# Idle matmuls in planned waits, padded loads of v and a new table of places in an attention and two-layer mixture kernel on one core

## The chip, the cores and the metric

The kernel runs on one NeuronCore of a Trainium2 chip, in one launch. The metric is the device time of that core in microseconds; the time before is the median of three runs. Five engines work side by side, each in its own program order: TensorE (PE; its weight loads are shown as PEld), VectorE (DVE), ScalarE (ACT), GpSimd (POOL) and SyncE (SP), which issues every DMA.

## What is computed

```python
def reference(q, k, v, moe_w_in, moe_w_out, moe_a, moe_b, moe2_phi, moe2_w1, moe2_w2):
    # attention, 4 x 8 heads, 576 positions, 64 wide:
    # means of 4 positions attend to each other (144 x 144), repeated 4 times,
    # plus attention over the positions less than 4 away
    x = (out_up + out_local).transpose(0, 2, 1, 3).reshape(2304, 512)
    h = x @ w_in                                   # 512 -> 2048
    P = a[0] + a[1] * h + a[2] * h**2 + a[3] * h**3
    Q = 1.0 + abs(b[0]) * abs(h) + abs(b[1]) * h**2
    x = (P / (Q + 1e-06)) @ w_out                  # 2048 -> 512
    # soft mixture of 8 experts with 4 slots each
    logits = x @ phi
    d, c = softmax(logits, 0), softmax(logits, 1)
    slots = d.T @ x                                # 32 x 512
    out = c @ [relu(slots[e] @ w1[e]) @ w2[e] for e in range(8)]
```

## The kernel before

**Stages.** Sixteen attention units (four batches, two heads side by side on the 128 partitions) come first. Each is a `pair`: banded scores of nine 64-row tiles (`sc0`, `sc1`), scores of the pooled heads (`scd`), the peak (DVE), the exponential (ACT), the norm, transposes of the probabilities (`tp0` to `tp2`, `td0`, `td1`), products with v (`avd`, `av`) and the sum `x`, split into a high and a low part (`XH`, `XL`). Four units make one `XH`/`XL` of 512 tokens. The first four units have buffers of their own (the four `Set`s); the other twelve take turns in set A. Between them, eight pieces of `w_in` are cut from 64-bit words by DVE and split into `W0` to `W7` (`split_in`), and eight of `w_out` likewise (`split_out`), stored to a scratch in HBM and folded with phi into `wphi`.

**The middle.** `h` multiplies a pair of `W` columns with 512 tokens (24 matmuls into two banks, `hps`, L757 of the profile), and eleven steps on ACT, DVE and POOL make the rational function of it (`ab`, `cr`, `v`, `a`, `t`, `p`, `ln`, `ex`, `e`, `nL`, `gL`, L819 to L842). The results are transposed (`tr`, L867) and copied out (`gc`, L608 on ACT or L610 on DVE) and summed into logits (`lg`). `route` does the softmax over tokens as it goes: `lt`, `tk`, and `dsp` (L939), which adds a group of tokens to the 32 slots.

**The end.** `sl` multiplies the slots with w_out (`Wo`), `l1` with the experts' w1 (`hp`, L1171), `l2` with w2 (`op`, L1292), and `o` combines. w1 and w2 come in 32 loads of 1 MB (`we`) into buffers of the middle, as these fall free, and 19 stores (`out`) end the program.

**What sets the order.** Every piece of work is entered by `at` with its reads, writes and PSUM bank. `Plan.order` sorts all of them by the table `PLACE` (one number for each piece), so the order on each engine is written in that table; the strings in `F` choose the engine of a piece (a for ACT, d for DVE, p for POOL), one letter for each unit or block. `order` also runs through the pieces with the costs in `PARTS` and keeps a clock of TensorE of its own (`fast`, `tick`), by which it hands out the three shared PSUM banks. SP's loads wait in SP's own order.

**What the change touches.** `F`, `PLACE`, `FILL` and `PARTS`; `order` and `emit` (L232 on); `load_v` (L416), which fetches v twice, as 72 rows for pooling (`vd`) and as 70 rows of windows (`vw`); `logits` (its bank `lg`); `fillers` (L1002), matmuls on a cleared tile, 44 of them, all ahead of the first `h`; `turn_c` and `keep_c`, the transposes of the combine weights late in the program; and in `kernel` the arrays `vw` and `vd`.

Of the kernel before, what the change touches and what calls it, by code (L numbers as in the profile page):

```python
# [29 lines left out]
    pq="ddppdddddddppppp",  # L30
    pk="ppddddppddpddddd",
    pv="pppppdpppppppppp",
    nl="dppppddpppppdppp",
    nd="dddppppddpdppdpp",
    wih="aaadaaaa",
    wil="pdpppppp",
    xh="aaaaadaadaaaddadd",
    xl="pdpdpppdppppddppd",
    v="ppddpppddpddpdppppdppdpppppddpppdppdp",
    e="ddddddddddddddddddddddddddddddddddddd",  # L40
    cr="adaaaadaaaaadaaaaaddaaaddaddaaaaaaaaa",
    a="daaaaaddaaaaaaadadaadadaadadaadaaadaa",
# [66 lines left out]
    cr=(407, 277, 451, 329, 528, 501, 627, 585, 675, 696, 735, 778, 819, 848, 882, 917, 939, 973, 998, 1053, 1088,
        1114, 1146, 1175, 1194, 1208, 1230, 1269, 1276, 1307, 1320, 1343, 1368, 1395, 1407, 1440, 1445),  # L110
    v=(412, 282, 483, 334, 538, 508, 632, 589, 681, 703, 739, 788, 824, 852, 888, 919, 945, 981, 1008, 1062, 1095,
        1122, 1153, 1178, 1196, 1214, 1232, 1274, 1282, 1312, 1325, 1348, 1373, 1403, 1412, 1447, 1450),
    a=(415, 262, 442, 467, 541, 535, 609, 623, 665, 720, 758, 774, 818, 851, 880, 918, 943, 965, 997, 1034, 1076,
        1108, 1154, 1173, 1193, 1213, 1229, 1245, 1268, 1301, 1321, 1337, 1359, 1380, 1405, 1433, 1453),
    t=(419, 266, 459, 473, 547, 540, 616, 641, 670, 728, 763, 780, 823, 861, 889, 921, 948, 982, 1014, 1047, 1085,
        1116, 1157, 1177, 1195, 1216, 1234, 1251, 1277, 1303, 1326, 1344, 1361, 1384, 1409, 1438, 1456),
    p=(424, 281, 465, 480, 576, 543, 635, 647, 685, 732, 768, 801, 834, 865, 896, 928, 957, 994, 1024, 1063, 1104,
        1119, 1163, 1182, 1198, 1217, 1236, 1258, 1286, 1315, 1328, 1347, 1367, 1386, 1413, 1449, 1466),
    ln=(422, 294, 485, 341, 546, 516, 645, 594, 686, 713, 743, 797, 828, 855, 900, 927, 953, 990, 1010, 1070, 1103,
        1130, 1158, 1185, 1200, 1218, 1240, 1279, 1284, 1324, 1331, 1353, 1385, 1411, 1419, 1451, 1455),  # L120
    ex=(426, 297, 489, 347, 550, 520, 649, 597, 689, 717, 749, 804, 833, 864, 903, 930, 960, 1002, 1021, 1077, 1117,
        1135, 1161, 1187, 1202, 1220, 1248, 1281, 1291, 1327, 1334, 1363, 1387, 1414, 1420, 1467, 1458),
# [30 lines left out]
    we=(1378, 1339, 1338, 1352, 1355, 1463, 1495, 1459, 1492, 1375, 1371, 1392, 1432, 1423, 1428, 1425, 1510, 1509,  # L153
        1487, 1496, 1488, 1528, 1521, 1527, 1518, 1526, 1534, 1536, 1530, 1539, 1535, 1533),
    zm=(1205,),
    gst=(1512,),
    inv=(1505,),
    gt0=(1513,),
    gt1=(1514,),
# [1258 lines left out]
```

## Time and profile before

| | |
|---|---|
| time, median of 3 runs | 556.72 us (555.61 to 557.39) |
| the profiled execution, its own time | 560.98 us |
| its span, first to last instruction | 558.9 us |
| mean granted TensorE clock | 0.935 |
| busy: PE, DVE, ACT, POOL | 499.3, 469.8, 331.6, 175.8 us |
| moved by DMA | 83.83 MB, 150 GB/s in the mean |

All durations below come from the profiled execution. [...] A busy PE is not PE at its peak, since the ends of matmuls are modelled.

### The profile page before, as it was taken

The numbers are of one execution on the slowest core, as the hardware profiler recorded it, in microseconds if no ns is written. First come the engines' busy times: TensorE is split into PE (matmuls) and PEld (weight loads), VectorE is DVE, ScalarE is ACT, GpSimd is POOL, SyncE is SP. The second block draws the span as 40 slices with busy tenths as digits, with TensorE's granted clock in tenths as the row PEclk, the third lists the DMA queues.
The fourth block names the chain that finished last, engine by engine and source line by source line (L and its number), as shares of the span: only waits on it lengthen the run. The fifth ranks groups of instructions, "written<-read, shape, count | busy, mean of one in ns | idle before, by whom it ended". The sixth has DMA issues, their size and how long they took to land.

```text
span 558.9 us, 10661 instructions
## 1 busy us (share of the span) xinstructions
PE 499.3 (89%) x4332; PEld 355.6 (64%) x4332; DVE 469.8 (84%) x618; ACT 331.6 (59%) x636; POOL 175.8 (31%) x130
## 2 busy tenths in 40 slices
PE   7799889678887979799999989999999999769995
PEld 4466667456665757576778767677775798323465
DVE  5687999889989899888999999999999999962523
ACT  4356554755774554877787665676658868820122
POOL 2637085537331151500254442243410313000100
PEclk9899997767996989989999999999999999789998
DMA  8986543221234543102002020024000096899977
GB/s 231 216 348 199 211 155 150 88 88 64 99 114 156 158 135 137 44 37 65 24 2 88 23 87 1 24 75 189 39 1 0 2 344 259 333 385 420 420 302 288
DMA packets 16705, 83.83 MB, mean 150 GB/s; under 512 B 1968, under 2 KB 2480, under 8 KB 10000
## 3 DMA queue, kind: packets, MB, share of 16 engines
q1 hardware_dynamic: 16656, 83.15, 42.4%
q8 instruction: 34, 0.56, 0.4%
q14 instruction: 15, 0.12, 0.1%
HBM read 74.23 MB, written 8.91 MB: 149 GB/s over the span
## 4 chain that ended last, share of the span: by engine, by line
PE 48%; DVE 28%; ACT 10%; DMA 9%; issue 3%; SPq 1%; POOL 0%; ACTq 0%; DVEq 0%
PE hps L757 19%; PE gt L867 4%; DMA at<-in_qk 3%; DVE gate L841 3%; PE dsp L939 3%; DVE wst L639 3%; DVE gate L825 3%; DMA at<-in_vd 2%; PE hp L1171 2%; PE sc L459 2%; PE lg L883 2%; PE op L1292 2%; DVE wo L643 2%; DVE gate L839 2%; DVE gate L842 2%
## 5 line engine op out<-in xcount | busy, mean ns | idle before, releaser
L757 PE MATMUL hps<-XH,W 128*128 128x512 f32 x512 | 177.1, 412 | 3.1 <-DVE A L836 2.1
L757 PEld LDWEIGHTS hps<-XH,W 128*128 128x128 f32 x512 | 99.7, 195 | 31.4 <-issue 3.9
L825 POOL TENSOR_TENSOR gate<-gate 128x1024 f32<-128x1024 f32 x23 | 59.5, 2589 | 158.7 <-ACT gate L819 112.0
L757 PE MATMUL hps<-XL,W 128*128 128x512 f32 x256 | 102.9, 402 | 0.0
L757 PEld LDWEIGHTS hps<-XL,W 128*128 128x128 f32 x256 | 49.9, 195 | 9.1
L837 ACT ACTIVATE gate<-gate,one 128x1024 f32<-128x1024 f32 (+1 forms) x37 | 41.9, 1131 | 22.5 <-POOL gate L825 16.6
L841 DVE SCALAR_TENSOR_TENSOR gate<-gate,one 128x1024 f32<-128x1024 f32 (+1 forms) x37 | 50.3, 1359 | 4.8 <-ACT gate L838 4.8
L828 ACT ACTIVATE gate<-hps 128x1024 f32<-128x1024 f32 (+1 forms) x37 | 37.2, 1005 | 18.8 <-PE hps L757 9.4
L482 ACT ACTIVATE at<-sc,at 128x70 f32<-128x70 f32 x144 | 32.9, 333 | 22.6 <-DVE at L476 12.7
L838 ACT ACTIVATE gate<-gate 128x1024 f32<-128x1024 f32 (+1 forms) x37 | 38.4, 1038 | 0.6
L497 POOL TENSOR_TENSOR at<-at 128x630 f32<-128x630 f32 (+1 forms) x21 | 25.1, 1194 | 39.4 <-DVE at L493 39.3
L608 ACT COPY G<-gt 128x512 f32<-128x512 f32 x53 | 30.7, 586 | 7.5 <-PE gt L867 7.3
L819 ACT ACTIVATE gate<-gate,cf_sb 128x1024 f32<-128x1024 f32 (+1 forms) x28 | 34.1, 1218 | 0.5
L842 DVE SCALAR_TENSOR_TENSOR gate<-gate 128x1024 f32<-128x1024 f32 x24 | 32.6, 1358 | 0.6
L839 DVE SCALAR_TENSOR_TENSOR gate<-gate,cf_sb 128x1024 f32<-128x1024 f32 x24 | 32.1, 1341 | 0.2
L502 PE MATMUL tp<-cf_sb,at 128*70 128x128 f32 x144 | 25.5, 307 | 6.6 <-DVE at L543 2.8
L505 ACT COPY at<-tp 70x512 f32<-70x512 f32 (+1 forms) x48 | 21.8, 476 | 16.1 <-PE tp L502 15.9
L836 DVE SCALAR_TENSOR_TENSOR gate<-gate,cf_sb,hps 128x1024 f32<-128x1024 f32 x24 | 30.6, 1275 | 0.4
L867 PE MATMUL gt<-cf_sb,gate 128*128 128x128 f32 x192 | 29.8, 286 | 1.2 <-DVE X L543 0.9
L459 PEld LDWEIGHTS sc<-at 64*64 64x64 f32 x576 | 22.0, 143 | 13.9 <-issue 9.2
L825 DVE TENSOR_TENSOR gate<-gate,hps 128x1024 f32<-128x1024 f32 x24 | 29.2, 1215 | 0.9 <-ACT gate L828 0.6
L459 PE MATMUL sc<-at 64*64 64x70 f32 x576 | 26.9, 238 | 3.1 <-DMA at<-in_qk 3.1
(158 smaller groups left out, 992.7 us busy)
## 6 DMA issues: line engine op xcount, KB each, us to landing
we<-in_w SPq DMA_DIRECT2D x32, 1024.0 KB
at<-in_qk SPq DMA_DIRECT2D x16, 579.0 KB
wst<-in_w_in SPq DMA_DIRECT2D x8, 1024.0 KB
wst<-in_w_out SPq DMA_DIRECT2D x8, 1024.0 KB
at<-in_vw SPq DMA_DIRECT2D x16, 315.0 KB
at<-in_vd SPq DMA_DIRECT2D x16, 288.0 KB
out<-late SPq DMA_DIRECT2D x17, 256.0 KB
wo_dram<-wo SPq DMA_DIRECT2D x8, 512.0 KB
```

The costliest lines, as they stand in the source:

```text
L459: nc.tensor.matmul(t[r, i - i0, :], lhsT=s.qT[r, 64 * i:64 * i + 64], rhs=s.kT[r, 64 * i:64 * i + WIN], start=False, stop=True, skip_group ...
L482: nc.scalar.activation(out=dst[:, i, :], in_=st["s", j][:, i, :], func=ACTF.Exp, scale=scale, bias=mx[:, i:i + 1], accum_out=sm[:, i:i + 1 ...
L757: nc.tensor.matmul(hps[m][:, c].rearrange("p u t -> p (u t)"), lhsT=W[p][:, w, kk, 128 * c:128 * c + 128], rhs=x[xx][:, kk, :], start=(kk ...
L819: act(out=out, in_=x, func=ACTF.Identity, scale=coef[:, w:w + 1], bias=coef[:, b:b + 1])
L825: (nc.vector if who == "d" else nc.gpsimd).tensor_tensor(out=out, in0=x, in1=y, op=ALU.mult)
L828: do("ab", "B", "H", lambda B, H: act(out=B, in_=H, func=ACTF.Abs))
L837: do("ln", "C", "B", lambda C, B: act(out=C, in_=B, func=ACTF.Ln, bias=one))
L838: do("ex", "C", "", lambda C: act(out=C, in_=C, func=ACTF.Exp, scale=-1.0))
L839: do("n", n, P + "C", lambda n, P, C: stt(out=n, in0=P, scalar=coef[:, 0:1], in1=C, op0=ALU.add, op1=ALU.mult), part="nL" if kept == "2" e ...
L841: do("e", "B", "C", lambda B, C: stt(out=B, in0=B, scalar=one, in1=C, op0=ALU.add, op1=ALU.mult), pick=("e", m))
L842: do("g", "A", "B" + n, lambda A, B, n: stt(out=A, in0=B, scalar=-2.0, in1=n, op0=ALU.add, op1=ALU.mult), part="gL" if n == "A" else "g")
L867: nc.tensor.transpose(gt[n][:, u, 128 * c:128 * c + 128], g_of(n, c)[:, 128 * u:128 * u + 128], idn)
```

## The change

1. **Idle matmuls.** `order` drops its clock of TensorE and counts matmuls at full speed after the first 5.3 us of the plan. Wherever the plan sees TensorE wait over 0.6 us, it notes a number of idle matmuls, (wait - 0.35) / 0.083, and `emit` puts them ahead of the waiting piece. Each is 128x192 in bf16 on a tile of zeros, adds to the upper half of the logits' bank, and waits for nothing. There are 245 (20 of them at the very start), for 44 of 128x512 before.
2. **v in 80 rows.** The arrays `vd` and `vw` get rows of zeros up to 80, and `load_v` fetches 80 rows. What is computed still reads 72 and 70.
3. **A new table.** `PLACE` has new numbers throughout, and `F` other engines for some pieces. DVE loses six `gc` copies, three `a`, two whole and two half `v` multiplies, two norm scalings, two `XH` casts, the casts of one `W` and of the last block's x, and that block's subtraction; it gains two `W` subtractions, two of `XL` and one pooling of v. ACT gets the copies, casts and `a`; POOL the `v` multiplies.
4. **Banks.** `LG` is one tile for the whole program, and `turn_c` takes one of the three shared banks, not the logits'.

```diff
 F = dict(
...
-    gc="aadadaadaaaaaaaaaaaaaaaaaddadaadaadaadadaaaadadaaaadaaaaaadaaaadadaaaddd",
+    gc="aaaadaaaaaaaaaaaadaaaaadaaaaaaddadadaaadaaaaaadaaaadaaaaaaaaaaaaaaaaaddd",
...
-    ldqk=(2, 3, 4, 7, 19, 161, 210, 271, 332, 378, 425, 549, 706, 777, 906, 1001),
+    ldqk=(2, 4, 5, 7, 21, 151, 213, 268, 325, 369, 407, 556, 698, 761, 893, 965),
...
-FILL = (12, 2, 4, 0, 8, 0, 2, 0, 0, 0, 8, 4, 4)
+FILL = (10,) + (0,) * 12
...
-    ldqk=dict(sp=1.7), ldv=dict(sp=2.3), ldi=dict(sp=2.8), ldo=dict(sp=2.8), sto=dict(sp=1.6), ldc=dict(sp=.5),
+    ldqk=dict(sp=1.8), ldv=dict(sp=3.0), ldi=dict(sp=2.8), ldo=dict(sp=2.8), sto=dict(sp=1.6), ldc=dict(sp=.5),
...
-                rows, now = self.rows.get(before, 1.0), t
-                while us > 1e-6:
-                    while tick <= now:
-                        fast, busy, tick = busy >= .42 * TICK, 0.0, tick + TICK
-                    rate = 1.0 if fast else 0.5
-                    step = min(us / rate, tick - now)
-                    now, us, busy = now + step, us - step * rate, busy + step * rate * rows
-                us = now - t
+                if t - free[e] > .6:
+                    self.idles[n] = int((t - free[e] - .35) / .083)
+                us *= 1.0 if t > 5.3 else 2.0
...
         for n in self.order(banks):
             self.now = self.place.get(n)
+            if n in self.idles:
+                self.idle(self.idles[n])
             self.items[n][5](*self.items[n][6])
...
+    LG = psum.tile([128, 2 * TB], F32, tag="lg", name="lg")
...
+            self.Vl, self.Vdl = v[0:80], self.Vd[0:80]
...
-        nc.sync.dma_start(out=s.Vd, in_=vd[bb, p])
-        nc.sync.dma_start(out=s.V, in_=vw[bb, p].rearrange("r (t c) -> r t c", t=9))
+        nc.sync.dma_start(out=s.Vdl, in_=vd[bb, p])
+        nc.sync.dma_start(out=s.Vl, in_=vw[bb, p])
...
-            nc.tensor.matmul(fill, lhsT=acc.bitcast(BF16)[:, 0:128], rhs=acc.bitcast(BF16)[:, 0:512], start=True, stop=True)
+            nc.tensor.matmul(fill[:, 0:192], lhsT=zero[:, 0:128], rhs=zero, start=not used, stop=True,
+                             skip_group_check=True)
+            used.append(n)
...
-        mid["c"] = psum.tile([128, 4, 128], F32, tag="lg", name="ct", bufs=1)
+        mid["c", u] = bank("ct", shape=(4, 128))
...
+    def rows80(x):
+        return np.pad(x, [(0, 0), (0, 0), (0, 80 - x.shape[2]), (0, 0)])
```

Three places of the order. **TensorE, in the attention units of the second batch**, ahead of the blocks that use `W2`: `av` is the product with v, `tp` and `tpd` are transposes of probabilities, `sc` and `scd` scores. Before:

```order
L529 MATMUL avd<-at 64x144 x4
L522 MATMUL avd<-at 64x64 x2
L522 MATMUL av<-at 64x64 x16
L502 MATMUL tp<-cf_sb,at 70x128 x8
L510 MATMUL tpd<-cf_sb,at 72x128 x6
```

and in the change:

```order
L526 MATMUL avd<-at 64x144 x4
L519 MATMUL avd<-at 64x64 x2
L519 MATMUL av<-at 64x64 x16
L1004 LDWEIGHTS zero
L1004 MATMUL lg<-zero 128x192
...
L499 MATMUL tp<-cf_sb,at 70x128 x4
L507 MATMUL tpd<-cf_sb,at 72x128 x3
```

Behind this `av` stand 39 idle matmuls, the longest run. From here to the first use of `W2` there are 24, 7, 4 and 25 more; in all, 61 stand ahead of the first `h` and 184 behind it.

**TensorE at the end of the middle**, where the last groups of tokens go to the slots (`dsp`), the sum is transposed (`gst`) and multiplied with w_out (`sl`). Before:

```order
L930 MATMUL tok<-cf_sb,L 128x32 x2
L939 MATMUL dsp<-G,DC 32x512 x8
L1111 MATMUL gst<-cf_sb,acc 128x128 x4
L1125 MATMUL sl<-Wo,GT 32x512 x16
L1143 MATMUL si<-cf_sb,GT 128x32 x4
```

and in the change:

```order
L927 MATMUL tok<-cf_sb,L 128x32 x2
L936 MATMUL dsp<-G,DC 32x512 x8
L1004 LDWEIGHTS zero
L1004 MATMUL lg<-zero 128x192
...
L1115 MATMUL gst<-cf_sb,acc 128x128 x4
L1004 LDWEIGHTS zero
L1004 MATMUL lg<-zero 128x192
...
L1129 MATMUL sl<-Wo,GT 32x512 x16
```

Ahead of this `dsp` stand 3, 15 and 5 idle matmuls, and behind it 7, 11, 5 and 3 up to the first expert matmul, where there was none.

**SP, the loads of the experts' weights** (`we`) and the reload of w_out (`Wo`). Before:

```order
L1044 DMA Wo<-wo_dram 128x2048 x4
L976 DMA we<-in_w 128x2048 x14
L980 DMA we<-in_w 128x2048 x2
L976 DMA we<-in_w 128x2048 x2
L980 DMA we<-in_w 128x2048 x14
```

and in the change:

```order
L973 DMA we<-in_w 128x2048
L1048 DMA Wo<-wo_dram 128x2048 x4
L973 DMA we<-in_w 128x2048 x13
L977 DMA we<-in_w 128x2048
L973 DMA we<-in_w 128x2048 x2
L977 DMA we<-in_w 128x2048 x15
```

One load of 1 MB moves ahead of the four of `Wo`; the other 31 keep their side of it.

## Rows read from the trace of the kernel before

**Rows 1.** The page: busy time of each engine; the granted clock in 40 slices.

```profile
PE 499.3 (89%) x4332; PEld 355.6 (64%) x4332; DVE 469.8 (84%) x618; ACT 331.6 (59%) x636; POOL 175.8 (31%) x130
...
PEclk9899997767996989989999999999999999789998
```

**Rows 2.** Stretches: us, PE, PEld, DVE, ACT, POOL busy, clock, DMA share, GB/s.

```profile
75.00:100.00 25.00, 22.31 (x215) 17.08 (x213) 22.56 (x32) 13.66 (x32) 15.43 (x11) 0.86 0.37 137
100.00:125.00 25.00, 16.87 (x183) 12.66 (x183) 21.73 (x33) 15.19 (x43) 11.55 (x7) 0.66 0.31 99
125.00:150.00 25.00, 20.74 (x161) 15.57 (x162) 24.16 (x32) 16.03 (x30) 16.20 (x11) 0.86 0.26 90
150.00:200.00 50.00, 41.56 (x299) 30.49 (x297) 43.93 (x45) 29.50 (x51) 11.02 (x7) 0.90 0.39 122
...
250.00:300.00 50.00, 50.00 (x400) 35.69 (x399) 45.48 (x57) 37.65 (x70) 12.53 (x10) 1.00 0.15 43
...
400.00:450.00 50.00, 49.70 (x306) 36.51 (x299) 49.02 (x47) 37.20 (x51) 9.95 (x5) 1.00 0.06 19
...
475.00:490.00 15.00, 12.14 (x90) 5.48 (x92) 14.15 (x19) 12.80 (x28) 0.00 (x0) 0.77 0.87 338
...
510.00:520.00 10.00, 8.98 (x85) 3.13 (x78) 2.81 (x9) 0.00 (x0) 1.85 (x1) 1.00 1.01 419
```

**Rows 3.** The chain that ended last, in order of time: start us, us, what.

```profile
3.46 13.45 DMA at<-in_vd
...
61.38 2.74 PE hps L757 x12
...
174.49 5.23 PE hps L757 x12
...
258.58 1.85 PE dsp L939 x16
...
317.96 3.26 DVE gate L842
...
481.35 3.64 PE dsp L939 x16
...
497.04 3.53 PE dsp L939 x16
```

**Rows 4.** Groups on DVE by shape: busy us, mean ns | idle before.

```profile
L842 DVE SCALAR_TENSOR_TENSOR gate<-gate 128x1024 f32<-128x1024 f32 x24 | 32.6, 1358 | 0.6
...
L825 DVE TENSOR_TENSOR gate<-gate 128x1024 f32<-128x1024 f32 x12 | 15.8, 1320 | 0.9 <-ACT gate L819 0.9
...
L610 DVE COPY G<-gt 128x512 f32<-128x512 f32 x19 | 13.0, 683 | 0.1
...
L821 DVE TENSOR_SCALAR gate<-hps,cf_sb 128x1024 f32<-128x1024 f32 x9 | 12.1, 1339 | 0.8 <-ACT gate L828 0.5 <-PE gt L867 0.2
...
L497 DVE TENSOR_TENSOR at<-at 128x432 f32<-128x432 f32 x7 | 6.9, 997 | 0.0
...
L613 DVE TENSOR_TENSOR XL<-at,XH 128x512 fp32r<-128x512 f32 x5 | 3.4, 674 | 0.0
...
L443 DVE TENSOR_REDUCE at<-at 72x256 f32<-72x1024 f32 x1 | 2.0, 1956 | 0.0
...
L613 DVE TENSOR_TENSOR W<-wst,W 128x1024 fp32r<-128x1024 f32 x1 | 1.2, 1216 | 0.0
```

**Rows 5.** The timeline of the start: one run of the old fillers.

```profile
16.73 1.90 PE L1004 MATMUL fill<-acc 128*128 128x512 bf16 x8
```

**Rows 6.** DMA of the first 30 us in 40 slices, and packets of the whole program.

```profile
GB/s 0 0 117 323 420 340 334 340 377 327 272 159 182 194 189 190 209 193 170 170 202 246 211 201 204 206 197 220 137 251 193 216 224 160 242 232 377 349 407 412
...
DMA packets 16705, 83.83 MB, mean 150 GB/s; under 512 B 1968, under 2 KB 2480, under 8 KB 10000
```

**Rows 7.** Short stretches, columns as in rows 2.

```profile
109.22:112.63 3.41, 3.20 (x29) 1.85 (x27) 3.38 (x4) 1.95 (x5) 1.59 (x1) 0.50 0.00 0
```

More of the change, by code (lines that the diff above doesn't have):

```diff
@@ L29 @@
 F = dict(
[L30 to L39, printed above, removed]
+    pq="pppddddpdddpppdd",
+    pk="pppdddpdddddddpd",
+    pv="pppppppppdpdpppp",
+    nl="dppdppdppppppppp",
+    nd="ppppdddddpppdppp",
+    wih="aaaaaaaa",
+    wil="pddppdpp",
+    xh="aaaaaaaaaadaaadda",
@@ L153 @@
[L153 to L159, printed above, removed]
-    sl=(1516,),
-    si0=(1519,),
-    si1=(1520,),
-    si=(1522,),
-    z=(1523,),
-    l1=(1524, 1525, 1529, 1531, 1532, 1537, 1542, 1545),
-    z2m=(1540,),
-    hs0=(1548,),
-    hs1=(1549,),
-    ht=(1552,),
@@ L185 @@
-    out=(1594, 1591, 1597, 1604, 1609, 1588, 1602, 1607, 1617, 1624, 1625, 1633, 1638, 1640, 1644, 1647, 1653, 1650,
-        1652),
+    dm=(0,),
+    ldqk=(2, 4, 5, 7, 21, 151, 213, 268, 325, 369, 407, 556, 698, 761, 893, 965),
+    ldc=(1, 3),
+    ldv=(6, 8, 11, 23, 122, 228, 289, 337, 379, 439, 589, 655, 837, 935, 990, 1090),
+    coef=(50,),
+    pq=(9, 17, 28, 61, 120, 198, 230, 291, 343, 390, 423, 567, 724, 844, 923, 1015),
+    pk=(13, 22, 33, 77, 123, 201, 236, 321, 346, 392, 428, 593, 751, 857, 948, 1059),
@@ new lines @@
+    wc0=(144, 237, 508, 546, 577, 629, 682, 716),
+    wt1=(150, 242, 498, 544, 580, 624, 685, 715),
+    wc1=(155, 245, 501, 548, 585, 626, 689, 719),
+    wp=(161, 261, 511, 549, 591, 632, 699, 721),
+    wpp=(167, 265, 514, 552, 594, 638, 702, 725),
+    wq=(187, 267, 534, 573, 596, 643, 705, 737),
+    wpc=(188, 272, 537, 576, 600, 646, 707, 749),
+    ldi=(14, 30, 27, 203, 216, 234, 271, 153),
+    wih=(149, 199, 232, 260, 332, 374, 411, 455),
+    wil=(156, 210, 241, 269, 336, 396, 417, 464),
@@ new lines @@
+    lgc=(764, 966, 1224, 1392, 1485),
+    lt=(771, 799, 987, 1018, 1229, 1256, 1400, 1432, 1486),
+    L=(782, 807, 994, 1027, 1244, 1266, 1410, 1445, 1489),
+    mx=(779, 803, 992, 1020, 1231, 1270, 1407, 1447, 1490),
+    al=(788, 822, 996, 1026, 1258, 1318, 1435, 1463, 1497),
+    E=(787, 808, 998, 1028, 1246, 1274, 1415, 1459, 1492),
+    ss=(790, 864, 1010, 1191, 1273, 1356, 1455, 1474, 1508),
+    tk=(798, 809, 1004, 1040, 1250, 1281, 1426, 1462, 1494),
+    dt=(800, 812, 1009, 1043, 1252, 1283, 1436, 1464, 1496),
@@ new lines @@
+    ds=(804, 817, 1012, 1109, 1269, 1300, 1439, 1469, 1498),
+    ac=(810, 827, 1023, 1118, 1277, 1343, 1450, 1495, 1499),
+    wor=(1179,),
+    h8=(1332, 1337, 1328, 1345, 1354, 1369, 1348, 1359, 1372, 1391, 1378, 1387, 1408, 1412, 1402, 1421),
+    we=(1160, 1323, 1325, 1376, 1352, 1452, 1482, 1449, 1479, 1375, 1364, 1399, 1401, 1418, 1427, 1431, 1501, 1500,
+        1484, 1478, 1487, 1522, 1519, 1524, 1520, 1517, 1518, 1523, 1525, 1527, 1530, 1529),
+    zm=(1350,),
+    gst=(1503,),
+    inv=(1509,),
@@ new lines @@
+    gt0=(1504,),
+    gt1=(1505,),
+    sl=(1507,),
+    si0=(1510,),
+    si1=(1511,),
+    si=(1512,),
+    z=(1513,),
+    l1=(1515, 1516, 1521, 1526, 1528, 1531, 1535, 1538),
+    z2m=(1533,),
+    hs0=(1541,),
+    hs1=(1542,),
+    ht=(1546,),
+    z2=(1550,),
+    c1=(1502,),
+    c2=(1506,),
+    c3=(1514,),
+    cs=(1532, 1539, 1537, 1545, 1548),
+    ct=(1534, 1543, 1540, 1549, 1551),
+    cc=(1536, 1547, 1544, 1554, 1553),
+    l2=(1552, 1555, 1556, 1557, 1558, 1559, 1561, 1562, 1560, 1563, 1565, 1567, 1569, 1571, 1577, 1587, 1579, 1592,
+        1599, 1605, 1607, 1609, 1614, 1616),
@@ L187 @@
+    os=(1564, 1590, 1619),
+    s4=(1566, 1595, 1621),
+    s4h=(1568, 1598, 1624),
+    s4l=(1570, 1604, 1625),
+    o=(1585, 1573, 1580, 1575, 1589, 1596, 1572, 1582, 1602, 1611, 1612, 1618, 1623, 1628, 1629, 1632, 1638, 1640,
+        1635),
+    out=(1591, 1583, 1594, 1581, 1597, 1606, 1600, 1603, 1610, 1620, 1617, 1626, 1631, 1633, 1637, 1641, 1644, 1646,
+        1645),
 )
 IDLE = (0, 0)
-FILL = (12, 2, 4, 0, 8, 0, 2, 0, 0, 0, 8, 4, 4)
+FILL = (10,) + (0,) * 12
 PIECES, SHORT = 2, 1
@@ L260 @@
     issues = dict(ldv=2, wor=4)
-    rows = dict(sc0=.75, sc1=.75, scd=.85, av=.65, avd=.5, lg=.8, lt=.65, o=.55, wp=.85, wq=.13, si=.13, ht=.13, tk=.07, tr=.8,
-                tp0=.8, tp1=.8, tp2=.8, td0=.8, td1=.8, wt0=.8, wt1=.8, ct=.8, gst=.8)
     wait = dict(pe=.2, act=.14, dve=.13, pool=.14, sp=0.0)
@@ L270, in order @@
         owner, moved, self.place = [None] * banks, 0.0, {}
-        fast, busy, tick, before, shared = False, 0.0, TICK, None, 0.0
+        before, shared, self.idles = None, 0.0, {}
         count = {}
@@ L998, in attn_moe_moe_kernel @@
     sets = [A, Set(1, "G0", "G1", "G2", "G3"), Set(2, "g0", "g1", "g2", "g3"), Set(3, "w4", "w5", "w6", "w7")]
-    fill = psum.tile([128, 512], F32, tag="lg", name="fill", bufs=1)
+    fill = LG[:, TB:]
+    used = []
+    zero = const.tile([128, 192], BF16, name="zero")
+    nc.vector.memset(zero, 0.0)
     def fillers(n):
         for _ in range(n):
-            nc.tensor.matmul(fill, lhsT=acc.bitcast(BF16)[:, 0:128], rhs=acc.bitcast(BF16)[:, 0:512], start=True, stop=True)
+            nc.tensor.matmul(fill[:, 0:192], lhsT=zero[:, 0:128], rhs=zero, start=not used, stop=True,
+                             skip_group_check=True)
+            used.append(n)
+    plan.idle = fillers
     nc.vector.memset(acc, 0.0)
     if FILL[0]:
-        at(-100, "DM", "dm", fillers, FILL[0], w=["lg"], scale=FILL[0])
+        at(-100, "DM", "dm", fillers, 2 * FILL[0], w=["id"], scale=FILL[0])
     def load_cb():
@@ L1274, in keep_c @@
         dst = room(7, [128, 16, 128], F32R)[:, u:u + n] if u < 16 else mid["ct"]
-        nc.scalar.copy(out=dst, in_=mid["c"][:, 0:n, :])
+        nc.scalar.copy(out=dst, in_=mid["c", u][:, 0:n, :])
     for j in range(5):
@@ L1280, in attn_moe_moe_kernel @@
         tail("cs", "cs", split_c, u, n, t=t, r=["DC", ("done", 4 if j == 0 else 5)], w=[("cs", j)])
-        tail("ct", "ct", turn_c, u, n, t=t, r=[("cs", j)], w=["lg"], scale=n / 4)
-        tail("cc", "cc", keep_c, u, n, t=t, r=["lg", ("done", 3), *(["L"] if j == 4 else [])], w=[("CT", j)])
+        tail("ct", "ct", turn_c, u, n, t=t, r=[("cs", j)], ps=("ct", j), scale=n / 4)
+        tail("cc", "cc", keep_c, u, n, t=t, r=[("ct", j), ("done", 3), *(["L"] if j == 4 else [])], w=[("CT", j)])
     so = {}
```

195 lines of the change are left out of this document (76 added, 119 removed), and 14 rows, old and new, of tables (gc, tr).

## The prediction

> **What bounds the kernel now.** I read the page first, then the stretches, then the chain. On the page [rows 1] TensorE is busy 89% of the span and VectorE 84%, ScalarE 59% and GpSimd 31%: two engines are near full, the other two have room. The clock row beside it says that a busy TensorE is not always a fast one: its lowest digits, 6 and 7, lie between the 7th and the 13th of the 40 slices (84 to 182 us) and at the 35th (475 us).
>
> The stretches [rows 2] tell who is the limit where. [...] From 250 to 450 us TensorE is busy all the time at full clock (50.00 of 50 us, and 49.70 at the end of it) with VectorE at 45.48 to 49.02 of 50: both are the limit, and no clock is left to win. From 475 to 490 the clock falls to 0.77. From 510 on DMA is full (share 1.01, 419 GB/s) with the experts' weights.
>
> [...]
>
> **The change part by part.** The sum is made against the profiled execution, 560.98 us, which lies 4.26 us (0.8%) above the median of 556.72 us and above all three timed runs; what I find is taken off the median.
>
> *Work taken off VectorE.* At the prices of [rows 4]: six copies of G at 0.683 (4.10), three linear steps at 1.339 (4.02), two `v` at 1.320 (2.64), two halves of it (1.32), two norm scalings, priced as the 432-element one, 0.997 (1.99), four casts at no more than the 0.674 of the `XL` row (2.70), and one subtraction like W's, 1.216: 18.0 us go. Two subtractions of W (2.43), two of XL (1.35) and one pooling of v (1.96) come: 5.7. Net 12.3 us of VectorE's 469.8, most of it between 75 and 490 us, where it bounds. ScalarE takes the copies and linear steps in its 41% of free time; that cover would be gone only where TensorE waits for a copied G. Gain between 0 (TensorE holds 250 to 450 us anyway) and 12.3; I take two thirds, **-8**, since in all stretches from 75 to 200 us VectorE is the fuller engine.
>
> *Clock in the middle.* [...] But the end gains at most what VectorE is idle there, 12.6 us, and part of those holes is other waiting. Between 0 and -12.6 I take the middle, **-6**; what is late next is VectorE, with W2 to W7 still to be cut.
>
> *Clock near the end.* Two `dsp` at 1.85 save 1.8 + 1.7 = 3.5 us, and both stand on the chain. Behind them the loads of weights limit: DMA is full at 510 us. The load that moves ahead of `Wo` takes 1 MB off that queue, 1.05 MB / 419 GB/s = 2.5 us. So between 0 (loads land no earlier) and -5.5 (3.5, and more from the transposes there) I take **-3**.
>
> *What the idle matmuls cost.* One old filler of 512 columns took 1.90 / 8 = 0.237 us at full clock [rows 5]; 192 columns by the same rate are 0.089 us, an estimate. The 61 ahead of the first `h` (5.4 us) replace 44 old ones (10.4 us). The 184 behind it are 16.4 us of work with no use. They wait for nothing, so they run in the wait that the plan saw, if it is there: the largest place, 39 + 24 + 7 + 4 + 25 = 99 of them, 8.8 us, lies in the stretch from 100 to 135 us, where TensorE was idle for 25 - 16.87 = 8.1 us in the first 25 us alone, and would be idle for more at full clock. In the last part some are tight: 11 of them are 1.0 us between `gst` and `sl`. Between 0 and +16.4 I take **+2**.
>
> *Loads of v.* The start waits for DMA: the chain has 13.45 us for a load of v [rows 3]. While the 128-row loads stand alone the core moves 320 to 420 GB/s; once v's 72 and 70 rows come, at about 8 us, it moves 160 to 250 [rows 6]. Two bounds for 80 rows. If the rate of the 128-row loads came back, the first four units' v (80 rows of 4096 and 4608 bytes each) would take 2.79 MB / 340 = 8.2 us instead of 2.47 MB / 200 = 12.3 for 72 and 70 rows: -4.1. If the rate stays, 0.32 MB more takes 1.6 us: +1.6. Eighty rows are far nearer to 72 than to 128, so I take **0**, the side on which the zeros cost no more than they bring. [...]
>
> *The table and the banks.* Which piece is late is new everywhere. An order can save or lose VectorE's idle time and no more than a like amount; from the 12.6 us above I give it 6 either way and take **0**. The bank of `turn_c` is nothing: those transposes lie between matmuls that DMA bounds.
>
> Sum: -8 - 6 - 3 + 2 + 0 + 0 = -15, or 546 us for such an execution as was profiled, and 556.7 - 15 = **542 us** for the median.
>
> **The rivals.**
> - *VectorE keeps the clock's gain* (chance 0.20). TensorE gets faster, but VectorE, full to 87 to 97% from 75 to 200 us, waits for its own loads and for GpSimd. For it: one multiplication in the chain took 3.26 us [rows 3] against a mean of 1.358 [rows 4], so VectorE can be held up, and more products now go to GpSimd. Against: the chain has slow matmuls in it. Then -8 - 1 + 2 remain: 549 us.
> - *All of it comes* (0.14): -12 - 8 - 4 + 1 - 2 = -25, 532 us.
> - *The idle matmuls stand in the way* (0.17, slower). TensorE takes its work in order; behind an idle run waits the `tp` or `h` that VectorE and ScalarE need next. Place: the 99 between the seventh unit's `av` and W2, and the 46 from the last `dsp`s to the experts. If the waits are not where the plan has them, 16.4 us are paid at full clock and near twice that at half, for 6 + 3 us of clock. It decides once more than the gain of VectorE's relief and the clock, 17 of 16 to 33 us, is paid. With 21 us paid: 556.7 - 17 + 21 = 561 us.
> - *The clock falls all the same and the rest evens out* (0.09, no change). From 109.2 to 112.6 us TensorE was busy for 3.20 of 3.41 us, with transposes, scores and small products, at clock 0.50 [rows 7]; no wait stood there, so the plan puts nothing there. Then -6 and -3 fall out, +2 stays, and of the relief 3 us, since slow TensorE work hides the rest: 555.7 us. [...]
>
> **How the numbers follow.** The forecast near 542 (537 to 547) has 0.40, the rivals 0.20, 0.14, 0.17 and 0.09. A measurement of this kernel can tell about 0.3%, 1.7 us, from no change. Faster: 0.40 + 0.20 + 0.14 and a little of the last, 0.75; the same 0.08; slower 0.17. The range leaves out the slower case and the far half of the best: 530 to 557 us.
>
> **What would show it.** Right: clock near 1.00 from 75 to 200 and from 475 to 500 us; all `dsp` at about 1.85 us; VectorE busy near 457 us; 245 idle matmuls at about 0.09 us, with TensorE's waits in front of W2 shorter by their time. The v loads still at 160 to 250 GB/s in the start. Wrong: clock digits under 9 again between 100 and 135 us; VectorE idle for more than 13 us from 75 to 200 us, behind TensorE; `sl` or the first `hp` starting only when idle matmuls end; or a DMA share of 1 for longer than before at the end, which would take the tail's 3 us.

## The result and the profile after

| | before | after |
|---|---|---|
| median | 556.46 us (4 runs, 555.61 to 557.39) | 535.41 us (4 runs, 531.26 to 539.37) |
| ratio | | 0.9596, 95% interval 0.9527 to 0.9666 |
| profiled execution | 560.98 us, span 558.9 | 539.37 us, span 537.3 |

The changed kernel is 21 us faster; 15 were forecast, and 535.4 lies in the range of 530 to 557. Two later sets of runs of the same kernel gave 0.9621 and 0.9607. The ratio leaves out one slow run of the four after, 539.37 us, which is also the profiled execution; the profiled one of before lies above all its timed runs too. All numbers below are from these executions unless a run is named; e1_after and e4_after are the changed kernel run again.

The page after: busy time of each engine, the granted clock in 40 slices, and the packets.

```profile
PE 492.9 (92%) x4533; PEld 365.2 (68%) x4533; DVE 461.2 (86%) x604; ACT 339.7 (63%) x649; POOL 179.3 (33%) x131
...
PEclk9899996989999998999999999999989999999998
...
DMA packets 17091, 85.13 MB, mean 158 GB/s; under 512 B 2064, under 2 KB 2576, under 8 KB 10384
```

VectorE lost 8.6 us of its busy time and ScalarE won 8.1 [rows 1]; in e1_after VectorE lost 11.5 (458.3). The stretches after, with the columns of [rows 2]:

```profile
75.00:100.00 25.00, 21.80 (x217) 17.50 (x211) 22.85 (x35) 14.66 (x39) 9.56 (x7) 0.80 0.36 123
100.00:125.00 25.00, 20.25 (x260) 17.02 (x257) 22.92 (x34) 15.79 (x35) 12.30 (x8) 0.93 0.32 85
125.00:150.00 25.00, 22.68 (x177) 17.23 (x176) 24.72 (x30) 16.07 (x32) 13.55 (x8) 1.00 0.26 86
150.00:200.00 50.00, 46.72 (x382) 35.36 (x382) 47.91 (x48) 36.04 (x64) 20.25 (x11) 1.00 0.50 159
...
475.00:490.00 15.00, 13.39 (x120) 6.80 (x122) 7.50 (x17) 3.34 (x10) 0.00 (x0) 1.00 0.99 414
```

From 100 to 200 us the clock is up from 0.66, 0.86 and 0.90 to 0.93, 1.00 and 1.00, and VectorE's idle time from 75 to 200 us fell from 12.6 to 6.6 us (4.0 in e1_after). From 75 to 100 us the clock is not held: 0.80 for 0.86 (0.93 in e1_after). So far this looks as the prediction had it; whether one made the other is what the experiments ask.

Groups on VectorE after, by shape, as in [rows 4]:

```profile
L836 DVE SCALAR_TENSOR_TENSOR gate<-gate,cf_sb 128x1024 f32<-128x1024 f32 x24 | 34.2, 1424 | 2.0 <-ACT gate L835 1.9
...
L822 DVE TENSOR_TENSOR gate<-gate 128x1024 f32<-128x1024 f32 x10 | 13.1, 1313 | 1.1 <-ACT gate L816 1.0
...
L607 DVE COPY G<-gt 128x512 f32<-128x512 f32 x13 | 8.9, 682 | 1.0 <-PE gt L864 1.0
...
L818 DVE TENSOR_SCALAR gate<-hps,cf_sb 128x1024 f32<-128x1024 f32 x5 | 6.7, 1341 | 1.9 <-ACT gate L825 1.9
```

The prices are those of before (0.682 for 0.683, 1.313 for 1.320, 1.341 for 1.339); only the counts moved. The chain of waits after (start us, us, what), its transfers up to 460 us and the turn to the experts:

```profile
4.02 13.95 DMA at<-in_qk
...
178.20 7.46 DMA wst<-in_w_out
...
478.44 1.97 PE dsp L936 x16
480.50 0.76 DVE acc L944
481.31 0.66 PE gst L1115 x4
481.96 0.91 PE lg L1004 x11
482.87 3.62 PE sl L1129 x32
486.51 0.48 ACT GT L1140
487.04 1.15 PE si L1147 x8
488.19 0.25 PE lg L1004 x3
```

The same chain of the kernel before has five transfers up to 460 us, 47.6 us in sum: the 13.45 us of [rows 3] and these four.

```profile
17.00 13.39 DMA at<-in_qk
...
48.18 5.52 DMA at<-in_qk
...
157.09 6.68 DMA wo_dram<-wo
...
184.97 8.54 DMA wst<-in_w_out
```

After, 21.4 us of transfers stand on it; in e1_after it is one of 12.24 us, in e4_after one of 6.89 us. So the sum varies between executions of one program, and a transfer on the chain tells what was waited for, not what its absence would save. The prediction had read the first of the five and not followed the chain to the next. In the last rows of after, 11 idle matmuls stand between `gst` and `sl` and 3 ahead of `hp`: 1.2 us on the chain, 0.083 us each.

The programs compared below differ by where their span goes, so I cut each at three points: the first `hps` matmul, the last one, and the first `hp` of the experts.

| profiled execution | to first `hps` | to last `hps` | to first `hp` | to the end | span |
|---|---|---|---|---|---|
| before | 61.1 | 414.4 | 32.8 | 50.5 | 558.9 |
| after | 55.8 | 403.9 | 28.9 | 48.6 | 537.3 |
| e1_after | 52.6 | 403.3 | 28.9 | 48.8 | 533.7 |
| e1_no_idle | 52.8 | 402.0 | 30.4 | 48.7 | 533.9 |
| e1_v72 | 55.1 | 400.8 | 28.9 | 48.7 | 533.5 |
| e1_act_back | 52.2 | 415.2 | 30.3 | 48.6 | 546.3 |
| e2_old_F_P_no_idle | 58.8 | 408.3 | 32.4 | 50.3 | 549.8 |
| e2_old_F_P_idle | 60.5 | 409.6 | 31.1 | 50.2 | 551.4 |
| e2_new_F_old_P | 57.6 | 436.4 | 33.5 | 50.6 | 578.2 |
| e2_old_F_new_P | 55.2 | 438.1 | 30.8 | 48.9 | 573.0 |
| e3_before_no_filler | 61.1 | 412.3 | 32.7 | 50.0 | 556.1 |
| e3_idle_x3 | 54.9 | 411.5 | 32.3 | 48.4 | 547.0 |
| e4_after | 56.0 | 400.4 | 28.9 | 48.9 | 534.2 |
| e4_replanned | 52.7 | 413.0 | 26.8 | 49.3 | 541.9 |

### The profile page after: what moved, and what is told of

The parts are those of the page before. It is cut to its first block, busy times and chain, and to the rows that moved or that the text cites. A ratio compares the mean times of both kernels' runs of the same rounds, so it can differ in the third digit from the quotient of the medians.

```text
span 537.3 us, 11081 instructions
## 1 busy us (share of the span) xinstructions
PE 492.9 (92%) x4533; PEld 365.2 (68%) x4533; DVE 461.2 (86%) x604; ACT 339.7 (63%) x649; POOL 179.3 (33%) x131
## 2 busy tenths in 40 slices
DMA packets 17091, 85.13 MB, mean 158 GB/s; under 512 B 2064, under 2 KB 2576, under 8 KB 10384
## 4 chain that ended last, share of the span: by engine, by line
PE 52%; DVE 30%; ACT 8%; issue 5%; DMA 4%; SPq 1%; POOL 0%; DVEq 0%; ACTq 0%
PE hps L754 21%; PE gt L864 5%; PE hps L765 3%; PE op L1296 3%; DVE wst L636 3%; DMA at<-in_qk 3%; PE lg L880 3%; DVE gate L822 3%; PE dsp L936 2%; PE hp L1175 2%; DVE gate L838 2%; DVE gate L836 2%; DVE at L489 2%; DVE gate L833 2%; ACT at L479 2%
## 5 line engine op out<-in xcount | busy, mean ns | idle before, releaser
L754 PE MATMUL hps<-XH,W 128*128 128x512 f32 x512 | 173.2, 407 | 4.5 <-DVE A L833 2.8
L754 PEld LDWEIGHTS hps<-XH,W 128*128 128x128 f32 x512 | 98.4, 192 | 31.1 <-issue 3.5
L822 POOL TENSOR_TENSOR gate<-gate 128x1024 f32<-128x1024 f32 (+1 forms) x27 | 65.3, 2422 | 153.8 <-ACT gate L816 117.7
L494 POOL TENSOR_TENSOR at<-at 128x630 f32<-128x630 f32 (+1 forms) x23 | 33.4, 1454 | 79.5 <-DVE at L490 60.9
L834 ACT ACTIVATE gate<-gate,one 128x1024 f32<-128x1024 f32 (+1 forms) x37 | 41.9, 1131 | 15.3 <-DVE gate L822 10.8
L838 DVE SCALAR_TENSOR_TENSOR gate<-gate,one 128x1024 f32<-128x1024 f32 (+1 forms) x37 | 48.7, 1320 | 0.2
L479 ACT ACTIVATE at<-sc,at 128x70 f32<-128x70 f32 x144 | 32.8, 332 | 24.4 <-DVE at L473 18.7
L605 ACT COPY G<-gt 128x512 f32<-128x512 f32 x59 | 34.0, 589 | 9.7 <-PE gt L864 9.7
L836 DVE SCALAR_TENSOR_TENSOR gate<-gate,cf_sb 128x1024 f32<-128x1024 f32 x24 | 34.2, 1424 | 2.0 <-ACT gate L835 1.9
L816 ACT ACTIVATE gate<-hps,cf_sb 128x1024 f32<-128x1024 f32 x19 | 23.0, 1209 | 13.9 <-PE gt L864 7.0
L839 DVE SCALAR_TENSOR_TENSOR gate<-gate 128x1024 f32<-128x1024 f32 x24 | 30.7, 1280 | 0.3
L456 PE MATMUL sc<-at 64*64 64x70 f32 x576 | 25.4, 230 | 4.7 <-DMA at<-in_qk 4.7
L456 PEld LDWEIGHTS sc<-at 64*64 64x64 f32 x576 | 20.7, 136 | 12.7 <-DMA at<-in_qk 5.9
```

The costliest lines, as they stand in the source:

```text
L456: nc.tensor.matmul(t[r, i - i0, :], lhsT=s.qT[r, 64 * i:64 * i + 64], rhs=s.kT[r, 64 * i:64 * i + WIN], start=False, stop=True, skip_group ...
L479: nc.scalar.activation(out=dst[:, i, :], in_=st["s", j][:, i, :], func=ACTF.Exp, scale=scale, bias=mx[:, i:i + 1], accum_out=sm[:, i:i + 1 ...
L754: nc.tensor.matmul(hps[m][:, c].rearrange("p u t -> p (u t)"), lhsT=W[p][:, w, kk, 128 * c:128 * c + 128], rhs=x[xx][:, kk, :], start=(kk ...
L816: act(out=out, in_=x, func=ACTF.Identity, scale=coef[:, w:w + 1], bias=coef[:, b:b + 1])
L822: (nc.vector if who == "d" else nc.gpsimd).tensor_tensor(out=out, in0=x, in1=y, op=ALU.mult)
L834: do("ln", "C", "B", lambda C, B: act(out=C, in_=B, func=ACTF.Ln, bias=one))
```

## The experiments

Theories: the time is VectorE's, and relief of it counts in full (VectorE); the clock that the idle matmuls hold is the gain, so that 6 to 11 us are lost without them (clock); the v loads are (loads); the order is (table).

**The changed kernel unaltered**, as the measure for the next three.

> The changed kernel again, unaltered, as the level for the others on the same chip: 535 us, ratio to before 0.953 to 0.967. If the spread of single runs (531 to 539 us) is the kernel's own, it shows again here.

534.93 us (534.38 to 535.7), ratio 0.9621 [0.9567, 0.9675]; before was 555.7 beside it.

**Without the planned idle matmuls.**

```diff
-            if n in self.idles:
-                self.idle(self.idles[n])
```

> The changed kernel without the 225 idle matmuls that the plan places (the 20 at the very start stay). [...] Rival, the table carries all of it: the clock falls but VectorE covers that, and the time stays within 2 us of the changed kernel, 533-537 us.

535.17 us, ratio 0.9642 [0.9568, 0.9716]: no change that the runs can tell. One of its four took 540.61 us; by the spread of four runs each, taking the idle matmuls out could cost up to 6 us or save up to 4. Its stretches (columns as above) and one step of its chain:

```profile
75.00:100.00 25.00, 16.45 (x193) 12.66 (x193) 24.29 (x38) 14.75 (x36) 11.93 (x9) 0.96 0.38 129
100.00:125.00 25.00, 18.34 (x174) 13.32 (x175) 23.24 (x34) 18.01 (x43) 11.30 (x8) 0.64 0.25 77
...
75.00:200.00 125.00, 104.74 (x940) 79.13 (x940) 120.64 (x144) 83.35 (x161) 52.33 (x33) 0.92 0.39 122
```

```profile
467.18 3.32 PE dsp L934 x16
```

and the same 75 to 200 us of e1_after:

```profile
75.00:200.00 125.00, 111.85 (x1067) 87.36 (x1067) 120.99 (x145) 84.81 (x168) 54.73 (x34) 0.97 0.39 125
```

The clock falls to 0.64 again between 100 and 125 us, where it is 0.93 in e1_after, and a `dsp` takes 3.32 us, nearly as before the change (0.66; 3.64 and 3.53 us). Yet VectorE is busy for 23.24 of those 25 us (22.92 in the kernel after), is idle for 4.4 us from 75 to 200 us where it is idle for 4.0 in e1_after, and the first `hp` starts at 485.2 us, in e1_after at 484.8. The matmuls do hold the clock (0.97 for 0.92 from 75 to 200 us), and up to the last `hps` that is worth nothing that shows: VectorE covers it. Behind the last `hps` they bring 1.5 us, their own time paid: 28.9 us to the first `hp` in all four executions of the new letters and table with them, 30.4 without. The clock theory, 6 to 11 us, falls for the new table.

**v loaded in 72 and 70 rows again.**

```diff
-        nc.sync.dma_start(out=s.Vdl, in_=vd[bb, p])
-        nc.sync.dma_start(out=s.Vl, in_=vw[bb, p])
+        nc.sync.dma_start(out=s.Vd, in_=vd[bb, p, 0:72])
+        nc.sync.dma_start(out=s.V, in_=vw[bb, p, 0:70].rearrange("r (t c) -> r t c", t=9))
```

> The changed kernel with the loads of v cut back to 72 and 70 rows (the arrays keep their rows of zeros, which are not fetched). By the forecast's value of 0 for the zeros: within 1 us of the changed kernel, with 200 GB/s while v is loaded as before. If 80 rows bring back the rate of the 128-row loads: 4 us slower, and the first 30 us move 235 GB/s instead of 267. [...]

534.89 us, ratio 0.9625 [0.955, 0.9699]: the same, though its four runs lie between 531.66 and 539.32 us, so that 1 us either way could not be seen. In the first 30 us the core moved 268 GB/s, with 80 rows 279 (e1_after); the difference is 0.3 MB, about the bytes of the padding. The rate of the 128-row loads did not come back, and the loads theory falls.

**Four kinds of pieces back on VectorE**, with the table and the numbers of idle matmuls kept.

```diff
-    wih="aaaaaaaa",
+    wih="aaadaaaa",
-    xh="aaaaaaaaaadaaadda",
+    xh="aaaaadaadaaaddadd",
-    a="adaaaadaaaaaaaaaadaaaaadaaaadadadadaa",
+    a="daaaaaddaaaaaaadadaadadaadadaadaaadaa",
...
+    gc="aadadaadaaaaaaaaaaaaaaaaaddadaadaadaadadaaaadadaaaadaaaaaadaaaadadaaaddd",
```

> The changed kernel with the engine letters of before for four kinds of work (copies of G, linear steps, XH and W casts), so that 13 pieces go back from ScalarE to VectorE, about 10 us of it; the table of places and the numbers of idle matmuls are held. Theory, VectorE's relief carries two thirds of its size: 6 to 8 us slower, 541-544 us. Rival, TensorE is the limit and VectorE has holes enough: at most 2 us slower.

546.38 us (545.09 to 548.16), ratio 0.9818 [0.9751, 0.9885]. The busy time in e1_after, then here:

```profile
PE 490.5 (92%) x4533; PEld 363.2 (68%) x4533; DVE 458.3 (86%) x604; ACT 339.2 (64%) x649; POOL 178.5 (33%) x131
```

```profile
PE 493.7 (90%) x4533; PEld 363.4 (67%) x4533; DVE 471.1 (86%) x617; ACT 329.6 (60%) x636; POOL 177.7 (33%) x131
```

VectorE is busy for 12.8 us more; the 13 pieces themselves are 10.8 us at the prices of [rows 4]. The median is 11.4 us longer, and in the profiled executions the stretch between the first and the last `hps` is 11.9 us longer. VectorE's idle time from 75 to 450 us is the same, 24.5 us for 23.8. So a microsecond on VectorE is nearly one on the end: relief counts almost in full, where I had taken two thirds. (These letters no longer fit the table that was made for others; what part of the 11.4 us is that misfit, no run shows.) 10 us of the 21 were still not accounted for, so the next four took letters (which engine does a piece, `F`) and table (in which order, `PLACE`) apart. All are the changed kernel's code. Below, one line of the old letters and one of the old table:

```diff
-    v="pppdppdpppdppppdpppdpdpppdpppddpdpppp",
+    v="ppddpppddpddpdppppdppdpppppddpppdppdp",
...
-    ldqk=(2, 4, 5, 7, 21, 151, 213, 268, 325, 369, 407, 556, 698, 761, 893, 965),
+    ldqk=(2, 3, 4, 7, 19, 161, 210, 271, 332, 378, 425, 549, 706, 777, 906, 1001),
...
```

**Both of before, no idle matmuls.**

> The changed kernel's code with the letters and the table of places of before, and no planned idle matmuls (the 20 at the start stay, the other old filler of 512 columns is gone too): what is left of the change is v padded to 80 rows and the bank of turn_c. VectorE theory (the time is VectorE's work and the order in which it comes; clock and padding bring nothing): 556, within 3 us of the kernel before. Clock theory: the filler ahead of the first h is gone with nothing in its place, so 558 to 564, with a lower clock than 0.935. If padding or bank did bring something: 550 or less.

552.95 us (10 runs), ratio 0.9937 [0.9904, 0.997]: a little faster than before, which no theory had.

**Both of before, with the idle matmuls that the plan then puts.**

> As e2_old_F_P_no_idle, but with the idle matmuls that the plan puts where it sees TensorE wait under the old letters and table (378, more than the 225 of the changed kernel). VectorE theory: the granted clock rises to about 0.97 and the time stays within 3 us of e2_old_F_P_no_idle, about 556. Clock theory: before, two dsp near the end stood on the chain at 3.6 and 3.5 us and hps at half speed, so the idle matmuls alone bring 6 to 12 us: 544 to 550.

550.58 us (10 runs), ratio 0.9894 [0.9862, 0.9927], clock 0.980 for 0.947. With the old table the idle matmuls (358, and 20 at the start) bring 2.4 us, not the 6 to 12 of the clock theory. The two intervals overlap a little, but both have the same runs of before in them; from the ten runs each, the gain lies between 1.4 and 4.7 us.

**New letters, old table.**

> The new letters (net about 12 us of work off VectorE) with the old table of places, no planned idle matmuls. If the letters alone bring the time (each us off VectorE is a us off the end, whatever the order): 544 to 546. If the letters bring it only in an order made for them: 551 to 560, with more idle time of VectorE than under either table with its own letters.

580.15 us, ratio 1.043 [1.0375, 1.0486].

**Old letters, new table.**

> The old letters with the new table of places, no planned idle matmuls. If the table by itself brings the 10 us that e1_act_back left unexplained (546.4 with most of VectorE's work back): 546 to 548. If the table is worth something only with its letters: 552 to 558. VectorE busy about 471 us in either case.

574.98 us, ratio 1.0323 [1.026, 1.0385]. Both miss, far on the slow side:

| no idle matmuls | old table | new table |
|---|---|---|
| old letters | 552.95 | 574.98 |
| new letters | 580.15 | 535.17 |

Either half alone costs 22 to 27 us, both together bring 17.8 (16.4 by the two ratios, since the right-hand lower cell ran beside other runs of before). How the time is lost differs. With the new letters in the old table VectorE has no more to do, but stands. This is 75 to 450 us (columns as above) of e2_old_F_P_no_idle, then of e2_new_F_old_P:

```profile
75.00:450.00 375.00, 339.97 (x2700) 253.53 (x2698) 352.38 (x402) 254.69 (x447) 133.39 (x84) 0.95 0.26 87
```

```profile
75.00:450.00 375.00, 331.39 (x2519) 243.44 (x2516) 323.32 (x374) 242.97 (x438) 130.74 (x76) 0.91 0.23 76
```

VectorE is idle for 51.7 us instead of 22.6. Eight GpSimd products now stand on the chain between 227 and 440 us, three of them over 3 us, where that of before has one and that of after none:

```profile
285.16 3.31 POOL gate L820
...
314.62 3.36 POOL gate L820
...
387.37 3.12 POOL gate L820
```

With the old letters in the new table VectorE is also idle for 33.1 us, and its own work grew: 480.2 us busy for 468.0, with the same 619 instructions. Two of its groups in e2_old_F_P_no_idle, then in e2_old_F_new_P:

```profile
L834 DVE SCALAR_TENSOR_TENSOR gate<-gate,cf_sb 128x1024 f32<-128x1024 f32 x24 | 32.1, 1341 | 0.2
...
L831 DVE SCALAR_TENSOR_TENSOR gate<-gate,cf_sb,hps 128x1024 f32<-128x1024 f32 x24 | 30.6, 1275 | 0.4
```

```profile
L834 DVE SCALAR_TENSOR_TENSOR gate<-gate,cf_sb 128x1024 f32<-128x1024 f32 x24 | 37.3, 1555 | 2.4 <-ACT gate L833 2.2
...
L831 DVE SCALAR_TENSOR_TENSOR gate<-gate,cf_sb,hps 128x1024 f32<-128x1024 f32 x24 | 30.6, 1273 | 1.6 <-ACT gate L823 1.2
```

The product that reads only SBUF tiles is longer, the one that reads `hps` (in PSUM) is not. The timeline of e2_old_F_new_P, GpSimd and then VectorE, shows why:

```profile
413.10 2.72 POOL L820 TENSOR_TENSOR gate<-gate 128x1024 f32<-128x1024 f32 x1 [8.41 <-ACT gate L814]
```

```profile
413.48 3.42 DVE L834 SCALAR_TENSOR_TENSOR gate<-gate,cf_sb 128x1024 f32<-128x1024 f32 x1
416.94 1.22 DVE L837 SCALAR_TENSOR_TENSOR gate<-gate 128x1024 f32<-128x1024 f32 x1
```

GpSimd's product ends at 415.82; VectorE's, begun at 413.48, ends 1.08 us later, at 416.90. It waited for GpSimd's to finish, and its 3.42 us count as busy. Of the products of 1024 columns with both inputs in SBUF, 26 in this trace begin while a product of GpSimd runs, and all 26 end 1.08 to 1.09 us behind it. Thirteen VectorE instructions with two tensor inputs take over 2.2 us in this trace, seven in that of e2_old_F_P_no_idle. That these waits and the longer standing make up the whole 22 us is argued from the traces; no run took either out.

**The old filler alone.** e2_old_F_P_no_idle also lacked 32 of the old fillers; here the kernel before lacks nothing else.

```diff
-FILL = (12, 2, 4, 0, 8, 0, 2, 0, 0, 0, 8, 4, 4)
+FILL = (12,) + (0,) * 12
```

> The kernel before with nothing changed but its old filler of 512 columns: the 12 at the start stay, the 32 others ahead of the first h go (8 us of TensorE by the 0.237 us of one at full clock). e2_old_F_P_no_idle was 0.6% faster than before, with padding, bank and this filler changed. If the filler is the cause: 553 to 554. If the padding or the bank is: 556 to 558, as before.

558.66 us (12 runs), ratio 0.9993 [0.9942, 1.0043]. Not the filler.

**Three times the idle matmuls at the same places.**

```diff
         self.end = end
+        self.idles = {115: 18, 69: 9, 36: 12, 151: 12, 308: 24, 131: 30, 318: 18, 413: 18, 421: 117, 621: 72,
...
+                      1367: 9, 1416: 45, 1477: 15, 1503: 21, 1507: 33, 1514: 15, 1516: 9}
         return done
```

> The changed kernel with three times the planned idle matmuls at the same 27 places (675 for 225, so 450 more, some 37 us at 0.083 us each; 98 of them in the last part, 8 us). If idle matmuls run only in waits that are there and VectorE covers the rest: up to 3 us above the changed kernel, 535 to 538. If TensorE's order makes every product behind them wait: from 75 to 200 us TensorE is idle for 13 us in the changed kernel and would be given some 20 us more, and the 8 us of the last part stand on the chain, so 543 to 555.

548.99 us, ratio 0.9883 [0.9819, 0.9946]: 14 us above the changed kernel for 37 us of extra matmuls. Its stretches and the turn of its chain:

```profile
100.00:125.00 25.00, 24.46 (x334) 22.81 (x332) 20.90 (x29) 12.48 (x27) 8.25 (x7) 1.00 0.21 63
125.00:150.00 25.00, 24.24 (x258) 19.96 (x256) 18.77 (x28) 15.97 (x30) 12.47 (x7) 1.00 0.17 53
```

```profile
489.53 2.72 PE lg L1005 x33
492.26 3.57 PE sl L1130 x32
```

TensorE is full and VectorE idle for 6.2 us in the second of these 25 us stretches, where it was idle for 0.3: the roles are turned round. So the rival in which idle matmuls stand in the way is real, from somewhere between one and three times the number that the plan puts.

**Letters and table moved on together**, by the plan's own count (85 letters, not the 75 of the expectation).

```diff
-    cr="adaaadaaaaadaddddaaaaaaaddaaaaaaaaaaa",
+    cr="aaaaadaaaadadadaadaadadaadaaaadaadaaa",
...
```

> The changed kernel with letters and table changed together: 75 letters and most places are moved by small steps that shorten the end that the kernel's own plan counts with its prices (the PARTS dict), by 8.9 us; the plan then puts 171 idle matmuls for 225. So far the plan's end ordered the five pairs of letters and table as the chip did (new 498 and 535; act_back 514 and 546; old 518 and 553; old letters in the new table 536 and 575; new letters in the old one 543 and 580). If letters and order together are what the change won by: 525 to 531. If the plan's prices are not fine enough for that: 533 to 540, with VectorE's idle time from 75 to 450 us no shorter than the 24 us of the changed kernel.

> The changed kernel again, unaltered, on the same chip as e4_replanned: 533 to 537.

548.77 us, ratio 0.9862 [0.98, 0.9923], beside 535.18 for the changed kernel (0.9607 [0.9559, 0.9655]). A miss: 8.9 us shorter in the plan, 13.6 us longer on the chip. Its chain has these transfers:

```profile
5.13 13.46 DMA at<-in_vd
18.61 15.09 DMA wst<-in_w_in
...
166.24 6.62 DMA wo_dram<-wo
...
192.41 6.70 DMA wo_dram<-wo
```

41.9 us of transfers, where e4_after has one of 6.89. The plan counts a store of `Wo` as 1.6 us of the queue and a load of W as 2.8; here they take 6.6 and 15.1. But the first two did not make the first `hps` late: it starts at 52.7 us, in e4_after at 56.0. The loss is between the first and the last `hps`, 413.0 for 400.4 us. There stand the two stores, and VectorE's busy time is 5.3 us longer (465.4 for 460.1), as in this group of e4_after, then of e4_replanned:

```profile
L839 DVE SCALAR_TENSOR_TENSOR gate<-gate 128x1024 f32<-128x1024 f32 x24 | 30.7, 1281 | 0.3
```

```profile
L839 DVE SCALAR_TENSOR_TENSOR gate<-gate 128x1024 f32<-128x1024 f32 x24 | 35.7, 1487 | 0.4
```

That stores and waits for GpSimd's products are what the plan does not count is read from the trace; no run took them out. No version here beats the changed kernel.

## Why the prediction was right, and where it was not

The forecast of 542 held by its size, and in part by luck: 9 of its 15 us came from the clock, which brings 1.5 us that can be seen in the changed kernel, while the relief of VectorE and the table brought more than it gave them.

- *Work off VectorE, -8: right in kind, undersized.* Pieces of 10.8 us put back cost 11.4 (e1_act_back). The count of 12.3 was good (VectorE's busy time fell by 11.5 us in e1_after) and so were its prices; "two thirds", for TensorE "busy all the time" from 250 to 450 us, was the error. The prediction read the first and the last of these stretches; in the two between, TensorE has 2.5 us of idle time each and VectorE is the fuller engine:

```profile
300.00:350.00 50.00, 47.51 (x379) 34.89 (x379) 47.69 (x59) 32.03 (x64) 21.64 (x15) 0.97 0.13 38
350.00:400.00 50.00, 47.49 (x362) 35.50 (x363) 47.92 (x51) 33.19 (x47) 18.09 (x11) 1.00 0.24 91
```

- *Clock, -6 and -3, with the idle matmuls' +2: 0.2 us in all, within the spread.* They hold the clock (0.93 for 0.64 from 100 to 125 us), but no run shows the -6 for the middle: the changed kernel without them took 535.17 us, with them 534.93. The failing step is the middle of the kernel, "the end gains at most what VectorE is idle there, I take the middle": VectorE's idle time from 75 to 200 us, 12.6 us before [rows 2], fell to 4.4 us without the clock and to 4.0 with it. Of the 3 us near the end, 1.5 came. In the order of before, all idle matmuls together bring 2.4 us. The first rival, that VectorE keeps the clock's gain, had this mechanism, but its 549 us (549.7 by its own sum) gave the letters and the table too little. The idle matmuls cost 1.2 us on the chain at the end, as one of the signs listed as wrong foresaw; three times as many cost 14 us.
- *Loads of v, 0: nothing speaks against it.* 534.89 against 534.93 us, with a spread of some us. The packets under 512 B are 2064 for 1968 [rows 6]; whether the padding brings or costs 1 us, four runs could not show. The rate stayed low while v came, as at most slots from the 12th to the 30th (154 to 253 GB/s) in this row of the first 30 us after:

```profile
GB/s 0 0 113 285 371 378 401 371 408 352 392 199 169 195 177 252 327 314 206 185 197 170 154 199 221 218 244 236 337 253 378 382 415 459 374 435 321 204 202 180
```

- *The table, 0 within 6: wrong.* "An order can save or lose VectorE's idle time and no more than a like amount" fails twice. The order also decides what is waited for ahead of 75 us: the first `hps` starts at 52.2 to 56.0 us in the eight executions with the new table, also with VectorE's work put back (52.2) or with all old letters (55.2), at 57.6 to 60.5 us in the three with the old table in the changed code, and at 61.1 us before. And it decides how long VectorE's products take, by what GpSimd does meanwhile, which counts as busy (1.555 us for 1.341 in the mean of one group of e2_old_F_new_P). The loss of 22 to 27 us for a table with the wrong letters shows how far 6 us was off as a bound.

Letters and table with no idle matmuls, 552.95 to 535.17, are 17.8 of the 21 us. As either without the other is a loss, these can't be divided between the two; 11.4 is what four kinds of letters are worth in the new table. The 3.5 us between before and the old letters and table in the new code (1.7 to 5.3 by its interval) stay open: it isn't the filler, and v's rows did nothing that could be seen in the new table, but neither they nor the transposes' bank, nor the plan without its clock of TensorE, which hands out the shared banks, were tried alone with the old one.

## What to carry to other kernels

Where an engine is full, work taken off it can be worth nearly its whole length (here 11.4 us for pieces of 10.8), and a slow clock on another engine nearly nothing while the full one covers it (here 0.2 us): ask which one covers the other before pricing the clock. Engines that take their work in order make the assignment of pieces and the order of pieces one decision; half of a good pair can be worse than neither (here by 22 to 27 us). Follow the chain to its second and third transfer, and test whether a transfer on it costs anything before pricing it. A plan that finds an order shorter can be wrong by more than its gain: confirm each order on the chip.

## What the runs showed of the hardware

In e2_old_F_new_P the 26 VectorE products of 1024 columns with two SBUF inputs that begin while a GpSimd product runs waited for it, to end 1.08 to 1.09 us behind it, and were recorded as busy while they waited: one took 3.42 us instead of about 1.28. The 3.26 us of the chain before [rows 3] was such a wait and no slow product: it ends 1.08 us behind a GpSimd product of 2.35 us that had begun 0.17 us ahead of it:

```profile
317.79 2.35 POOL L825 TENSOR_TENSOR gate<-gate 128x1024 f32<-128x1024 f32 x1 [6.40 <-ACT gate L819]
```

The `SCALAR_TENSOR_TENSOR` products of 1024 columns with an operand in PSUM took 1.22 to 1.28 us in all these traces, also the 16 of them that begin beside a running GpSimd product in e2_old_F_new_P.

The 225 idle matmuls of the plan raised the mean granted clock from 0.953 (e1_no_idle) to 0.974 (e1_after), from 0.64 to 0.93 in the stretch from 100 to 125 us, and the time did not change by more than the runs' spread (534.93 for 535.17 us).
